# Gating GpSimd's v copy and relu(k) on VectorE's reciprocal and product of three heads back, with new instruction lists and more PE warm-up, in a linear-attention kernel

## The chip, the cores and the metric

The kernel runs on one core of one Trainium2 chip. The metric is device time in microseconds (us), the median of several executions. All comparisons below use runs that were marked as fast runs (e5 and e7 have one slow execution each, which is left out of their medians); where the profiled execution of a kernel fell in a slow run, the text says so. Engines are named as in the profile: PE is TensorE, DVE is VectorE, ACT is ScalarE, POOL is GpSimd, SP is the engine that issues the DMAs.

Each execution has a time and a span (first to last instruction), and in every execution of this case the time is 1.8 us above the span: 179.61 against 177.8 for the profiled execution of the kernel before, 187.68 against 185.9 for that of the changed one.

## The reference

Linear attention without a mask, 32 heads, sequence 2048, head size 128, bf16:

```python
def reference(q, k, v):                       # q, k, v: (1, 32, 2048, 128), bf16
    phi_q = jnp.where(q > 0, q + 1, jnp.exp(q)) + 1e-6
    phi_k = jnp.where(k > 0, k + 1, jnp.exp(k)) + 1e-6
    kv = jnp.einsum("bhsd,bhse->bhde", phi_k, v)
    z = jnp.einsum("bhsd->bhd", phi_k)
    num = jnp.einsum("bhqd,bhde->bhqe", phi_q, kv)
    den = jnp.einsum("bhqd,bhd->bhq", phi_q, z)[..., None] + 1e-6
    return num / den
```

The kernel uses phi(x) = (min(exp(x), 1) + eps) + relu(x), so that both parts go to PE as separate matmuls.

## The kernel before

Every operation has a name and a head number, and five lists give the order on each engine. The lists are what the scheduler would be in other kernels; an engine takes its list strictly in order, and semaphores are derived from the dependencies. The operations of head h that the argument needs are:

| name | engine | what | two-port mode |
|---|---|---|---|
| ek, eq | ACT | exp(k), exp(q transposed) | - |
| em | DVE | min(exp k, 1) + eps, 128x2048 bf16, SBUF to SBUF | yes |
| emq | DVE | the same for q | yes |
| rkd | DVE | relu(k), first half, 128x1024 bf16, SBUF to SBUF | yes |
| rqb | DVE | relu(q) second half, from PSUM | no |
| r.0, f.0 | DVE | reciprocal and product of 12 row tiles, from PSUM | no |
| r.1, f.1 | DVE | the same for the last 4 tiles | no |
| rkp | POOL | relu(k), second half, SBUF to SBUF | - |
| v1 | POOL | copy of v beside a column of ones, SBUF to SBUF | - |
| T, kv, n | PE | transpose of q; phi(k) times v; phi(q) times kv | - |

Code of the parts that the change and the argument touch (cuts are marked):

```python
WARM = (60, 30)                              # PE warm-up groups w0, w1
def kv_parts(h):
    return WHOLE                             # kv of a head is one operation
def gate(name, h):
    return []                                # no gates
# ... (lists: a stretch of DVE's, head 12 to 13)
#   ... r12.0 f12.0 emq13.0 rkd15.0 em15.0 r12.1 rqb14 f12.1 rkd16.0 r13.0 emq14.0 f13.0 ...
#   ... (POOL's: heads are swapped in places)
#   ... rkp15.0 rkp14.0 v115.0 rkp16.0 v117.0 v116.0 rkp17.0 rkp18.0 v119.0 v118.0 ...
for i, (a, b) in enumerate(rkp_parts(h)):
    add("POOL", f"rkp{h}.{i}", lambda e, a=a, b=b: e.tensor_scalar(
        rk_sb[:, h % NR, a:b], k_sb[:, h % NI, a:b], BIG, 0.0, op0=ALU.min, op1=ALU.max),
        over("ldk", h, k_parts, a, b) + freed(NR, h, ("kv", kv_parts)) + gate("rkp", h))
for i, (a, b) in enumerate(v_parts(h)):
    add("POOL", f"v1{h}.{i}", lambda e, a=a, b=b: e.tensor_copy(
        v1_sb[:, h % NV, a:b, 0:D].bitcast(i32), v_sb[:, h % NI, a:b].bitcast(i32)),
        [f"ldv{h}.{i}"] + freed(NV, h, ("kv", kv_parts)) + gate("v1", h))
# ... (f.0: the product, one input from PSUM)
e.tensor_tensor(out=..., in0=_ap(o_ps, ...), in1=_ap(rden_sb, ...), op=ALU.mult)
```

Without a gate, a POOL operation of head h waits for its load and for kv of head h - 2 (two buffers), so it starts when PE ends that kv.

Of the kernel before, what the change touches and what calls it, by code (L numbers as in the profile page):

```python
# [8 lines left out]
ENGINES = ("PE", "DVE", "ACT", "POOL", "SP")  # L9
NH = 32  # L10
NI, NO, NE, NR, NV, NQ, NK = 7, 12, 2, 2, 2, 2, 2
WARM = (60, 30)
HALVES = ((0, 8), (8, 16))
WHOLE = ((0, 16),)

# [6 lines left out]


def kv_parts(h):
    return WHOLE


RKP = (8, 8, 8, 8, 8, 8, 8, 8, 8, 8, 8, 8, 8, 8, 8, 8, 8, 8, 8, 8, 8, 8, 8, 8, 8, 8, 8, 8, 8, 8, 8, 8)
# [23 lines left out]


def gate(name, h):
    return []


ORDER = {
    "PE": """
        T0.0 T0.1 w1 w0 T1.0 kv0.0 kv1.0 n0.0 n0.1 T2.0 kv2.0 n1.0 T3.0 n1.1 kv3.0 n2.0 T4.0 n2.1 kv4.0 n3.0 T5.0  # L60
        n3.1 kv5.0 n4.0 T6.0 n4.1 kv6.0 n5.0 n5.1 T7.0 kv7.0 n6.0 T8.0 n6.1 kv8.0 n7.0 T9.0 n7.1 kv9.0 n8.0 T10.0
        n8.1 kv10.0 n9.0 T11.0 n9.1 kv11.0 n10.0 T12.0 n10.1 kv12.0 n11.0 T13.0 n11.1 kv13.0 n12.0 T14.0 n12.1
        kv14.0 n13.0 T15.0 n13.1 kv15.0 n14.0 T16.0 n14.1 kv16.0 n15.0 T17.0 n15.1 kv17.0 n16.0 n16.1 T18.0 kv18.0
        n17.0 T19.0 n17.1 kv19.0 n18.0 T20.0 n18.1 kv20.0 n19.0 T21.0 n19.1 kv21.0 n20.0 T22.0 n20.1 kv22.0 n21.0
        T23.0 n21.1 kv23.0 n22.0 T24.0 n22.1 kv24.0 n23.0 n23.1 T25.0 kv25.0 n24.0 T26.0 n24.1 kv26.0 n25.0 T27.0
        n25.1 kv27.0 n26.0 T28.0 n26.1 kv28.0 n27.0 T29.0 n27.1 kv29.0 n28.0 T30.0 n28.1 kv30.0 n29.0 T31.0 n29.1
        kv31.0 n30.0 n30.1 n31.1 n31.0 n31.2
    """,
    "DVE": """
        v1ones0 rkd0.0 em0.1 rkd1.0 rqb0 em0.0 eps0 em1.0 emq0.1 emq0.0 rqb1 v1ones1 eps1 rkd2.0 eps2 ones emq1.0  # L70
        rkd3.0 em2.0 r0.0 f0.0 em3.0 rqb2 r0.1 rkd4.0 f0.1 r1.0 emq2.0 f1.0 em4.0 rkd5.0 r1.1 rqb3 f1.1 r2.0 f2.0
        emq3.0 em5.0 rkd6.0 rqb4 r2.1 f2.1 r3.0 emq4.0 f3.0 em6.0 r3.1 rqb5 rkd7.0 f3.1 r4.0 emq5.0 f4.0 em7.0 r4.1
        f4.1 rqb6 r5.0 f5.0 emq6.0 rkd8.0 em8.0 r5.1 rqb7 f5.1 r6.0 emq7.0 f6.0 rkd9.0 em9.0 r6.1 rqb8 f6.1 r7.0
        emq8.0 f7.0 rkd10.0 em10.0 r7.1 rqb9 f7.1 r8.0 emq9.0 f8.0 rkd11.0 em11.0 r8.1 rqb10 f8.1 r9.0 rkd12.0 f9.0
        emq10.0 em12.0 r9.1 rqb11 f9.1 r10.0 f10.0 emq11.0 em13.0 rkd13.0 r10.1 rqb12 f10.1 rkd14.0 r11.0 emq12.0
# [137 lines left out]
def bass_standalone__linear_attn_elu__prompt_kernel(nc: bass.Bass, q: bass.AP, k: bass.AP, v: bass.AP, out: bass.AP):  # L213
# [11 lines left out]
    with ExitStack() as es:  # L225
# [73 lines left out]
        def head(h):  # L299
# [153 lines left out]
```

## Time and profile before

The kernel before took 176.82 us (median of 3).

These are lines of its page: the span, the busy time of the engines, the DMA rows of the 40 slices, and the shares of the chain of waits that ended last, by engine.

```profile
span 177.8 us, 6416 instructions
...
PE 161.9 (91%) x2842; PEld 158.1 (89%) x2842; DVE 158.4 (89%) x266; ACT 154.4 (87%) x131; POOL 71.5 (40%) x71
...
DMA  5999999999999999999999999999999945999973
GB/s 171 323 407 416 411 404 406 412 404 410 408 406 409 406 417 411 407 411 417 412 417 414 420 414 416 416 414 417 412 405 418 414 196 183 285 417 412 418 313 120
...
PE 43%; DVE 20%; DMA 18%; issue 5%; SPq 4%; ACT 4%; POOL 3%; DVEq 0%; POOLq 0%
```

DMA is full from the 3rd slice to the 32nd, has a hole from the 33rd to the 35th (142 to 156 us, deepest up to 152), and is full again for three slices. The chain runs through PE, DVE and DMA; no single engine owns it.

Next, the busy time of each engine in three stretches (us from the start; the columns are named in the first line).

```profile
core 0: us, PE busy (x) PEld busy (x) DVE busy (x) ACT busy (x) POOL busy (x), PEclk, DMA share, GB/s
31.00:78.00 47.00, 47.00 (x857) 46.77 (x855) 46.16 (x80) 47.00 (x40) 21.36 (x21) 1.00 1.03 409
78.00:126.00 48.00, 45.15 (x808) 44.13 (x806) 46.85 (x76) 44.83 (x38) 20.78 (x19) 1.00 1.03 415
142.00:152.00 10.00, 9.21 (x169) 9.11 (x168) 10.00 (x19) 9.04 (x8) 4.15 (x4) 1.00 0.59 202
```

From 31 to 78 us PE and ACT are busy the whole time and DVE 46.2 of 47 us. In this stretch eq starts every 4.72 us; this is the pace that PE and ACT set. From 78 to 126 us PE falls to 45.2 of 48.

The hole in DMA has its cause in the DMA list. This is SP's timeline at the place: the store of head 25 stood early in the list, and everything behind it waited 15.7 us.

```profile
132.63 15.72 SPq L388 DMA_DIRECT2D out_dram<-la  x2
```

The three two-port operations of DVE, by shape: count, then busy us and mean ns.

```profile
L311 DVE TENSOR_SCALAR la<-la 128x2048 bf16<-128x2048 bf16 x31 | 22.5, 725 | 1.7 <-ACT la L308 1.7
L345 DVE TENSOR_SCALAR la<-la 128x2048 bf16<-128x2048 bf16 x31 | 21.5, 694 | 0.4 <-ACT la L343 0.4
...
L314 DVE TENSOR_SCALAR la<-la 128x1024 bf16<-128x1024 bf16 x32 | 18.0, 566 | 7.4 <-DMA la<-in_k_dram 7.3
```

What these means hide is seen in the timeline. Below are DVE's operations at 90 us (start, duration, then the operation) and POOL's one at the same time. They are emq15, em17, rkd17 and r14.1, and on POOL rkp18.

```profile
89.46 0.68 DVE L345 TENSOR_SCALAR la<-la 128x2048 bf16<-128x2048 bf16 x1
90.06 0.69 DVE L311 TENSOR_SCALAR la<-la 128x2048 bf16<-128x2048 bf16 x1
90.66 1.26 DVE L314 TENSOR_SCALAR la<-la 128x1024 bf16<-128x1024 bf16 x1
91.85 0.17 DVE L373 RECIPROCAL la<-la 128x4 f32<-128x4 f32 x1
```

```profile
90.57 1.08 POOL L318 TENSOR_SCALAR la<-la 128x1024 bf16<-128x1024 bf16 x1 [2.31 <-PE la L329]
```

POOL's rkp18 came up while em17 ran, 0.09 us before rkd17 started. It went in first, and rkd17, which takes 0.33 us from its start to the next start when alone, took 1.19. I call an em, emq or rkd *blocked* if it was dispatched (its record in the trace begins) during a POOL operation and took over 0.15 us more than its usual start-to-start time (0.60 us, 0.33 us for the 1024-element ones). The kernel before has 11 of them, 7.5 us in all. The small table sums up what bounds it.

| | measured |
|---|---|
| pace of PE and ACT | 4.72 us per head |
| DVE's eight operations of a head, unblocked, start to start | 4.63 us |
| DVE's slack per head | under 0.1 us |
| blocked DVE operations | 11, 7.5 us |
| hole in DMA | 142 to 152 us, 202 GB/s in place of 410 |

### The profile page before, as it was taken

The page shows a single profiled execution, that of the slowest core. Times are in us where ns is not written, and L with a number is a line of the kernel's source. Part 1 is how long each engine was busy: PE and PEld are TensorE (multiplying, and loading weights), DVE is VectorE, ACT ScalarE, POOL GpSimd, SP SyncE. Part 2 cuts the span into 40 slices and gives each one's busy share as a digit, 9 for nine tenths or more (in the row PEclk, how much of TensorE's full clock was granted, in tenths as well). Part 3 has the DMA queues.
Part 4 walks back from the last instruction along what each step waited for, and adds up shares of the span by engine and source line. Part 5 has one row for each costly group of instructions (what it writes and reads, how often), then busy time and mean ns, then how long its engine had stood idle before and what let it go on. Part 6 is the DMA issues. An engine that isn't in the chain of part 4 may idle for free.

```text
span 177.8 us, 6416 instructions
## 1 busy us (share of the span) xinstructions
PE 161.9 (91%) x2842; PEld 158.1 (89%) x2842; DVE 158.4 (89%) x266; ACT 154.4 (87%) x131; POOL 71.5 (40%) x71
## 2 busy tenths in 40 slices
PE   2986999999999999999889999988999989999870
PEld 1976999999999999999789999978999889989770
DVE  0156899999999999998999999999999999989973
ACT  2599799999999999999898999978999979994600
POOL 1253818417454246262723626264256424360000
PEclk9999999999999999999999999999999999999968
DMA  5999999999999999999999999999999945999973
GB/s 171 323 407 416 411 404 406 412 404 410 408 406 409 406 417 411 407 411 417 412 417 414 420 414 416 416 414 417 412 405 418 414 196 183 285 417 412 418 313 120
DMA packets 19179, 67.52 MB, mean 380 GB/s; under 512 B 2128, under 2 KB 2512, under 8 KB 19152
## 3 DMA queue, kind: packets, MB, share of 16 engines
q1 hardware_dynamic: 19152, 67.12, 95.1%
q8 instruction: 22, 0.36, 0.8%
q14 instruction: 5, 0.04, 0.1%
HBM read 50.33 MB, written 16.78 MB: 377 GB/s over the span
## 4 chain that ended last, share of the span: by engine, by line
PE 43%; DVE 20%; DMA 18%; issue 5%; SPq 4%; ACT 4%; POOL 3%; DVEq 0%; POOLq 0%
PE la L329 17%; DMA la<-in_k_dram 11%; PE la L364 9%; PE la L366 8%; PE la L340 8%; DVE la L380 8%; DMA out_dram<-la 7%; SPq L296 4%; DVE la L314 4%; DVE la L311 3%; DVE la L352 2%; ACT la L343 2%; DVE la L345 2%; POOL la L318 2%; POOL la L322 2%
## 5 line engine op out<-in xcount | busy, mean ns | idle before, releaser
L380 DVE TENSOR_TENSOR la<-la 128x1536 bf16<-128x1536 f32 (+2 forms) x65 | 77.7, 1199 | 2.0 <-DMA out_dram<-la 1.4
L366 PE MATMUL la<-la 128*128 128x129 bf16 x512 | 69.2, 222 | 0.0
L364 PE MATMUL la<-la 128*128 128x129 bf16 x512 | 69.1, 221 | 0.0
L329 PE MATMUL la<-la 128*128 128x129 bf16 x1024 | 64.0, 219 | 2.0 <-ACT la L349 1.4
L343 ACT ACTIVATE la<-la 128x2048 bf16<-128x2048 bf16 (+1 forms) x33 | 60.1, 1825 | 6.5 <-PE la L366 6.0
L308 ACT ACTIVATE la<-la 128x2048 bf16<-128x2048 bf16 (+1 forms) x33 | 61.3, 1860 | 2.1 <-DMA la<-in_k_dram 1.9
L329 PEld LDWEIGHTS la<-la 128*128 128x128 bf16 x1024 | 59.9, 97 | 2.7 <-DVE la L278 1.5
L318 POOL TENSOR_SCALAR la<-la 128x1024 bf16<-128x1024 bf16 x32 | 36.1, 1137 | 44.1 <-PE la L329 33.5
L322 POOL COPY la<-la 128x1024 int32<-128x1024 int32 (+1 forms) x33 | 35.3, 1076 | 44.0 <-PE la L329 22.4
L366 PEld LDWEIGHTS la<-la 128*128 128x128 bf16 x512 | 50.0, 98 | 0.0
L364 PEld LDWEIGHTS la<-la 128*128 128x128 bf16 x512 | 47.8, 98 | 0.0
L340 PE MATMUL la<-la 128*128 128x128 bf16 x512 | 34.8, 222 | 7.0 <-DMA la<-in_q_dram 3.6
L340 PEld LDWEIGHTS la<-la 128*128 128x128 bf16 x512 | 29.6, 99 | 9.0 <-issue 4.0
L359 PE MATMUL la<-la 128*128 128x3 bf16 (+1 forms) x192 | 32.6, 170 | 2.5 <-DVE la L380 2.5
L349 ACT ACTIVATE la<-la 128x1024 bf16<-128x1024 bf16 x32 | 32.6, 1019 | 2.5 <-PE la L340 2.5
L311 DVE TENSOR_SCALAR la<-la 128x2048 bf16<-128x2048 bf16 (+1 forms) x33 | 23.3, 706 | 3.1 <-ACT la L308 3.1
L314 DVE TENSOR_SCALAR la<-la 128x1024 bf16<-128x1024 bf16 x32 | 18.0, 566 | 7.4 <-DMA la<-in_k_dram 7.3
L345 DVE TENSOR_SCALAR la<-la 128x2048 bf16<-128x2048 bf16 (+1 forms) x33 | 22.3, 677 | 0.4 <-ACT la L343 0.4
L359 PEld LDWEIGHTS la<-la 128*128 128x128 bf16 x192 | 18.9, 99 | 3.5 <-DVE la L380 3.1
L352 DVE TENSOR_SCALAR la<-la 128x1024 bf16<-128x1024 bf16 x32 | 21.3, 667 | 0.7 <-ACT la L343 0.7
L373 DVE RECIPROCAL la<-la 128x12 f32<-128x12 f32 (+2 forms) x65 | 12.8, 198 | 2.2 <-PE la L366 1.4
L334 ACT ACTIVATE la<-la 128x129 bf16<-128x129 f32 x32 | 9.0, 281 | 1.0 <-PE la L329 1.0
(14 smaller groups left out, 13.5 us busy)
## 6 DMA issues: line engine op xcount, KB each, us to landing
la<-in_k_dram SPq DMA_DIRECT2D x31, 512.0 KB, 13.9
la<-in_q_dram SPq DMA_DIRECT2D x31, 512.0 KB, 13.9
la<-in_v_dram SPq DMA_DIRECT2D x31, 512.0 KB, 13.3
out_dram<-la SPq DMA_DIRECT2D x31, 512.0 KB, 13.2
la<-in_q_dram SPq DMA_DIRECT2D x2, 256.0 KB, 3.0
la<-in_k_dram SPq DMA_DIRECT2D x2, 256.0 KB, 5.2
la<-in_v_dram SPq DMA_DIRECT2D x2, 256.0 KB, 7.6
out_dram<-la SPq DMA_DIRECT2D x2, 192.0 KB, 2.1
```

The source lines that it names most:

```text
L308: add("ACT", f"ek{h}.{i}", lambda e, a=a, b=b: e.activation(em_sb[:, h % NE, a:b], k_sb[:, h % NI, a:b], ACT.Exp), [f"ldk{h}.{i}"] + freed ...
L311: add("DVE", f"em{h}.{i}", lambda e, a=a, b=b: e.tensor_scalar(em_sb[:, h % NE, a:b], em_sb[:, h % NE, a:b], 1.0, EPS, op0=ALU.min, op1=AL ...
L318: add("POOL", f"rkp{h}.{i}", lambda e, a=a, b=b: e.tensor_scalar(rk_sb[:, h % NR, a:b], k_sb[:, h % NI, a:b], BIG, 0.0, op0=ALU.min, op1=A ...
L322: add("POOL", f"v1{h}.{i}", lambda e, a=a, b=b: e.tensor_copy(v1_sb[:, h % NV, a:b, 0:D].bitcast(i32), v_sb[:, h % NI, a:b].bitcast(i32)), ...
L329: ins = e.matmul(kv_ps, lhsT=src[:, j], rhs=v1_sb[:, h % NV, j, 0:NC], start=(j + part == 0), stop=(j == NT - 1 and part == 1))
L340: ins = e.transpose(xT[:, j], q_sb[:, h % NI, j], ident[:])
L343: add("ACT", f"eq{h}.{i}", lambda e, a=a, b=b: e.activation(emq_sb[:, h % NQ, a:b], xT[:, a:b], ACT.Exp), [f"T{h}.{i}"] + freed(NQ, h, ("n ...
L349: add("ACT", f"rqa{h}", lambda e: e.activation(rq_sb[:, h % NQ, 0:n], xT[:, 0:n], ACT.Relu), over("T", h, q_parts, 0, n) + freed(NQ, h, (" ...
L359: e.matmul(_ap(o_ps[:, :], o + D, [[NC, m]]), lhsT=ones[:], rhs=epsr[:, 0:m], start=True, stop=False, skip_group_check=True)
L364: e.matmul(to, lhsT=emq_sb[:, h % NQ, t], rhs=kvs_sb[:, h % NK], start=False, stop=False, skip_group_check=True)
L366: ins = e.matmul(to, lhsT=rq_sb[:, h % NQ, t], rhs=kvs_sb[:, h % NK], start=False, stop=True, skip_group_check=True)
L380: return e.tensor_tensor(out=_ap(o_sb[:, :, :, :], first(o_sb[:, h % NO, t0, 0:1]) - first(o_sb[:, :, :, :]), [[m * D, nb], [D, m], [1, D] ...
```

## The change

Intent: let GpSimd work while VectorE reads PSUM. The v copy of head h now waits for r.0 of head h - 3, just before the long product f.0; relu(k) waits for f.0. The instruction lists were made anew for that (ACT's, not shown, changes only in heads 0 to 2 and 21), kv was halved, and four short warm-up groups of PE replace one of 30. The diff, cut to its core:

```diff
-WARM = (60, 30)
+WARM = (60, 15, 15, 15, 15)
 def kv_parts(h):
-    return WHOLE
+    return HALVES
 def gate(name, h):
-    return []
+    if h < 3:
+        return []
+    return [f"r{h - 3}.0"] if name == "v1" else [f"f{h - 3}.0"]
 ORDER = {
   "PE":                                        # (cut: kv halves, n0.0 before kv1)
-        T0.0 T0.1 w1 w0 T1.0 kv0.0 kv1.0 n0.0 n0.1 T2.0 kv2.0 n1.0 T3.0 n1.1 ...
+        w3 w4 T0.0 w1 T0.1 w2 w0 T1.0 kv0.0 kv0.1 n0.0 kv1.0 kv1.1 n0.1 T2.0 ...
   "DVE":                                       # (cut: heads 11 to 13 of 32)
-        ... r11.0 emq12.0 f11.0 em14.0 r11.1 rqb13 f11.1 r12.0 f12.0 emq13.0 rkd15.0 em15.0 r12.1 rqb14 f12.1 ...
+        ... r11.0 rkd14.0 emq12.0 f11.0 em14.0 r11.1 rqb13 f11.1 r12.0 emq13.0 f12.0 rkd15.0 em15.0 rkd16.0 rqb14 ...
   "POOL":                                      # (cut: now in the order of heads)
-        ... rkp15.0 rkp14.0 v115.0 rkp16.0 v117.0 v116.0 rkp17.0 ...
+        ... rkp14.0 v115.0 rkp15.0 v116.0 rkp16.0 v117.0 rkp17.0 ...
   "SP":                                        # (cut: stores and loads nearly in the order of heads)
-        ... st15.0 ldk30.0 st17.0 ldv29.0 ldq29.0 st18.0 st25.0 ldv30.0 ldk31.0 st16.0 ldv31.0 st21.0 ldq31.0 ...
+        ... st14.0 st15.0 ldv29.0 ldk30.0 ldq30.0 ldk31.0 ldq31.0 st16.0 ldv30.0 st17.0 ldv31.0 st18.0 st19.0 ...
```

More of the change, by code (lines that the diff above doesn't have):

```diff
@@ L54, in gate @@
 def gate(name, h):
-    return []
+    if h < 3:
+        return []
+    return [f"r{h - 3}.0"] if name == "v1" else [f"f{h - 3}.0"]
 ORDER = {
     "PE": """
-        T0.0 T0.1 w1 w0 T1.0 kv0.0 kv1.0 n0.0 n0.1 T2.0 kv2.0 n1.0 T3.0 n1.1 kv3.0 n2.0 T4.0 n2.1 kv4.0 n3.0 T5.0
-        n3.1 kv5.0 n4.0 T6.0 n4.1 kv6.0 n5.0 n5.1 T7.0 kv7.0 n6.0 T8.0 n6.1 kv8.0 n7.0 T9.0 n7.1 kv9.0 n8.0 T10.0
-        n8.1 kv10.0 n9.0 T11.0 n9.1 kv11.0 n10.0 T12.0 n10.1 kv12.0 n11.0 T13.0 n11.1 kv13.0 n12.0 T14.0 n12.1
-        kv14.0 n13.0 T15.0 n13.1 kv15.0 n14.0 T16.0 n14.1 kv16.0 n15.0 T17.0 n15.1 kv17.0 n16.0 n16.1 T18.0 kv18.0
-        n17.0 T19.0 n17.1 kv19.0 n18.0 T20.0 n18.1 kv20.0 n19.0 T21.0 n19.1 kv21.0 n20.0 T22.0 n20.1 kv22.0 n21.0
-        T23.0 n21.1 kv23.0 n22.0 T24.0 n22.1 kv24.0 n23.0 n23.1 T25.0 kv25.0 n24.0 T26.0 n24.1 kv26.0 n25.0 T27.0
-        n25.1 kv27.0 n26.0 T28.0 n26.1 kv28.0 n27.0 T29.0 n27.1 kv29.0 n28.0 T30.0 n28.1 kv30.0 n29.0 T31.0 n29.1
-        kv31.0 n30.0 n30.1 n31.1 n31.0 n31.2
+        w3 w4 T0.0 w1 T0.1 w2 w0 T1.0 kv0.0 kv0.1 n0.0 kv1.0 kv1.1 n0.1 T2.0 kv2.0 kv2.1 n1.0 T3.0 n1.1 kv3.0 kv3.1
+        n2.0 T4.0 n2.1 kv4.0 kv4.1 n3.0 n3.1 T5.0 kv5.0 kv5.1 n4.0 T6.0 n4.1 kv6.0 kv6.1 n5.0 T7.0 n5.1 kv7.0 kv7.1
+        n6.0 T8.0 n6.1 kv8.0 kv8.1 n7.0 T9.0 n7.1 kv9.0 kv9.1 n8.0 T10.0 n8.1 kv10.0 kv10.1 n9.0 T11.0 n9.1 kv11.0
+        kv11.1 n10.0 T12.0 n10.1 kv12.0 kv12.1 n11.0 T13.0 n11.1 kv13.0 kv13.1 n12.0 T14.0 n12.1 kv14.0 kv14.1 n13.0
+        T15.0 n13.1 kv15.0 kv15.1 n14.0 T16.0 n14.1 kv16.0 kv16.1 n15.0 T17.0 n15.1 kv17.0 kv17.1 n16.0 T18.0 n16.1
+        kv18.0 kv18.1 n17.0 T19.0 n17.1 kv19.0 kv19.1 n18.0 T20.0 n18.1 kv20.0 kv20.1 n19.0 T21.0 n19.1 kv21.0
+        kv21.1 n20.0 T22.0 n20.1 kv22.0 kv22.1 n21.0 T23.0 n21.1 kv23.0 kv23.1 n22.0 T24.0 n22.1 kv24.0 kv24.1 n23.0
+        T25.0 n23.1 kv25.0 kv25.1 n24.0 T26.0 n24.1 kv26.0 kv26.1 n25.0 n25.1 T27.0 kv27.0 kv27.1 n26.0 T28.0 n26.1
+        kv28.0 kv28.1 n27.0 T29.0 n27.1 kv29.0 kv29.1 n28.0 T30.0 n28.1 kv30.0 kv30.1 n29.0 n29.1 T31.0 kv31.0
+        kv31.1 n30.0 n30.1 n31.0 n31.1 n31.2
@@ L68 @@
     """,
     "DVE": """
-        v1ones0 rkd0.0 em0.1 rkd1.0 rqb0 em0.0 eps0 em1.0 emq0.1 emq0.0 rqb1 v1ones1 eps1 rkd2.0 eps2 ones emq1.0
-        rkd3.0 em2.0 r0.0 f0.0 em3.0 rqb2 r0.1 rkd4.0 f0.1 r1.0 emq2.0 f1.0 em4.0 rkd5.0 r1.1 rqb3 f1.1 r2.0 f2.0
-        emq3.0 em5.0 rkd6.0 rqb4 r2.1 f2.1 r3.0 emq4.0 f3.0 em6.0 r3.1 rqb5 rkd7.0 f3.1 r4.0 emq5.0 f4.0 em7.0 r4.1
-        f4.1 rqb6 r5.0 f5.0 emq6.0 rkd8.0 em8.0 r5.1 rqb7 f5.1 r6.0 emq7.0 f6.0 rkd9.0 em9.0 r6.1 rqb8 f6.1 r7.0
-        emq8.0 f7.0 rkd10.0 em10.0 r7.1 rqb9 f7.1 r8.0 emq9.0 f8.0 rkd11.0 em11.0 r8.1 rqb10 f8.1 r9.0 rkd12.0 f9.0
@@ L75 @@
-        emq10.0 em12.0 r9.1 rqb11 f9.1 r10.0 f10.0 emq11.0 em13.0 rkd13.0 r10.1 rqb12 f10.1 rkd14.0 r11.0 emq12.0
-        f11.0 em14.0 r11.1 rqb13 f11.1 r12.0 f12.0 emq13.0 rkd15.0 em15.0 r12.1 rqb14 f12.1 rkd16.0 r13.0 emq14.0
-        f13.0 em16.0 r13.1 rqb15 f13.1 r14.0 f14.0 emq15.0 em17.0 rkd17.0 r14.1 rqb16 f14.1 r15.0 rkd18.0 f15.0
-        emq16.0 em18.0 r15.1 f15.1 rqb17 r16.0 f16.0 emq17.0 em19.0 rkd19.0 r16.1 rqb18 f16.1 r17.0 emq18.0 f17.0
-        rkd20.0 em20.0 r17.1 rqb19 f17.1 r18.0 f18.0 emq19.0 rkd21.0 em21.0 r18.1 rqb20 f18.1 r19.0 emq20.0 f19.0
@@ L80 @@
-        em22.0 rkd23.0 rkd22.0 rqb21 r19.1 r20.0 f19.1 f20.0 emq21.0 em23.0 rkd24.0 rqb22 r20.1 f20.1 r21.0 emq22.0
-        f21.0 em24.0 rqb23 r21.1 f21.1 r22.0 emq23.0 rkd25.0 f22.0 em25.0 r22.1 f22.1 rqb24 r23.0 f23.0 emq24.0
-        rkd26.0 em26.0 r23.1 rqb25 f23.1 r24.0 emq25.0 f24.0 em27.0 rkd27.0 r24.1 rqb26 f24.1 r25.0 emq26.0 f25.0
-        rkd28.0 em28.0 r25.1 rqb27 f25.1 r26.0 emq27.0 f26.0 rkd29.0 em29.0 r26.1 rqb28 f26.1 r27.0 emq28.0 f27.0
-        rkd30.0 em30.0 r27.1 rqb29 f27.1 r28.0 f28.0 emq29.0 rkd31.0 em31.0 rqb30 r28.1 f28.1 r29.0 emq30.0 f29.0
@@ L85 @@
-        emq31.0 r29.1 rqb31 r30.0 f29.1 f30.0 r30.1 f30.1 r31.1 f31.1 r31.0 r31.2 f31.0 f31.2
+        eps0 rkd0.0 emq0.1 rkd1.0 v1ones0 rqb0 eps1 ones em0.0 em0.1 emq0.0 em1.0 v1ones1 eps2 r0.0 rkd2.0 rqb1 f0.0
+        em2.0 rkd3.0 emq1.0 em3.0 rkd4.0 r0.1 rqb2 f0.1 r1.0 f1.0 emq2.0 em4.0 rqb3 r1.1 f1.1 rkd5.0 r2.0 emq3.0
+        f2.0 em5.0 r2.1 f2.1 rqb4 r3.0 emq4.0 f3.0 rkd6.0 em6.0 rqb5 r3.1 f3.1 r4.0 emq5.0 f4.0 rkd7.0 em7.0 r4.1
+        rqb6 f4.1 r5.0 f5.0 emq6.0 em8.0 rkd8.0 r5.1 rqb7 f5.1 r6.0 rkd9.0 emq7.0 f6.0 em9.0 rqb8 r6.1 f6.1 r7.0
@@ new lines @@
+        rkd10.0 f7.0 emq8.0 em10.0 rqb9 r7.1 f7.1 r8.0 rkd11.0 emq9.0 f8.0 em11.0 r8.1 rqb10 f8.1 rkd12.0 r9.0
+        emq10.0 f9.0 em12.0 rqb11 r9.1 f9.1 rkd13.0 r10.0 emq11.0 f10.0 em13.0 r10.1 rqb12 f10.1 r11.0 rkd14.0
+        emq12.0 f11.0 em14.0 r11.1 rqb13 f11.1 r12.0 emq13.0 f12.0 rkd15.0 em15.0 rkd16.0 rqb14 r12.1 f12.1 r13.0
+        emq14.0 f13.0 em16.0 rkd17.0 rqb15 r13.1 f13.1 r14.0 emq15.0 f14.0 em17.0 rqb16 r14.1 f14.1 rkd18.0 r15.0
+        emq16.0 f15.0 em18.0 r15.1 rqb17 f15.1 r16.0 rkd19.0 emq17.0 f16.0 em19.0 rqb18 r16.1 f16.1 r17.0 emq18.0
@@ new lines @@
+        f17.0 rkd20.0 em20.0 r17.1 rqb19 f17.1 r18.0 rkd21.0 f18.0 emq19.0 em21.0 rqb20 r18.1 f18.1 r19.0 rkd22.0
+        emq20.0 f19.0 em22.0 rqb21 r19.1 f19.1 r20.0 rkd23.0 emq21.0 f20.0 em23.0 r20.1 rqb22 f20.1 emq22.0 r21.0
+        rkd24.0 f21.0 em24.0 r21.1 rqb23 f21.1 r22.0 emq23.0 f22.0 em25.0 rkd25.0 r22.1 rqb24 f22.1 r23.0 rkd26.0
+        f23.0 emq24.0 em26.0 r23.1 rqb25 f23.1 rkd27.0 r24.0 f24.0 emq25.0 em27.0 r24.1 f24.1 rqb26 r25.0 emq26.0
+        f25.0 rkd28.0 em28.0 rqb27 r25.1 f25.1 emq27.0 r26.0 rkd29.0 f26.0 em29.0 r26.1 rqb28 f26.1 r27.0 f27.0
@@ L86 @@
+        emq28.0 rkd30.0 r27.1 rqb29 f27.1 r28.0 em30.0 emq29.0 f28.0 r28.1 f28.1 rqb30 em31.0 rkd31.0 r29.0 f29.0
+        emq30.0 rqb31 r29.1 emq31.0 f29.1 r30.0 f30.0 r30.1 f30.1 r31.0 f31.0 r31.1 f31.1 r31.2 f31.2
     """,
     "ACT": """
-        rqa0 ek0.1 ek0.0 eq0.1 eq0.0 ek1.0 eq1.0 kvs0 rqa1 ek2.0 kvs1 ek3.0 eq2.0 kvs2 rqa2 ek4.0 eq3.0 kvs3 rqa3
+        rqa0 eq0.0 eq0.1 ek0.0 ek0.1 ek1.0 eq1.0 kvs0 ek2.0 rqa1 kvs1 ek3.0 eq2.0 kvs2 rqa2 ek4.0 eq3.0 kvs3 rqa3
         ek5.0 eq4.0 kvs4 rqa4 ek6.0 eq5.0 kvs5 rqa5 ek7.0 eq6.0 kvs6 rqa6 ek8.0 eq7.0 kvs7 rqa7 ek9.0 eq8.0 kvs8
@@ L92 @@
         ek18.0 eq17.0 kvs17 rqa17 ek19.0 eq18.0 kvs18 rqa18 ek20.0 eq19.0 kvs19 rqa19 ek21.0 eq20.0 kvs20 rqa20
-        ek22.0 eq21.0 rqa21 kvs21 ek23.0 eq22.0 kvs22 rqa22 ek24.0 eq23.0 kvs23 rqa23 ek25.0 eq24.0 kvs24 rqa24
+        ek22.0 eq21.0 kvs21 rqa21 ek23.0 eq22.0 kvs22 rqa22 ek24.0 eq23.0 kvs23 rqa23 ek25.0 eq24.0 kvs24 rqa24
         ek26.0 eq25.0 kvs25 rqa25 ek27.0 eq26.0 kvs26 rqa26 ek28.0 eq27.0 kvs27 rqa27 ek29.0 eq28.0 kvs28 rqa28
@@ L97 @@
     "POOL": """
-        ident0 ident rkp0.0 rkp1.0 v10.1 v10.0 v11.0 v12.0 rkp2.0 rkp3.0 v13.0 v14.0 rkp5.0 rkp4.0 v15.0 rkp6.0
-        v16.0 v17.0 v18.0 rkp7.0 rkp8.0 rkp9.0 v19.0 rkp10.0 v110.0 rkp11.0 v111.0 v112.0 rkp13.0 rkp12.0 v113.0
-        v114.0 rkp15.0 rkp14.0 v115.0 rkp16.0 v117.0 v116.0 rkp17.0 rkp18.0 v119.0 v118.0 rkp19.0 rkp20.0 v121.0
-        v120.0 rkp21.0 v122.0 rkp23.0 rkp22.0 v123.0 rkp24.0 v124.0 v125.0 v126.0 rkp25.0 rkp26.0 rkp27.0 v127.0
-        rkp28.0 v128.0 rkp29.0 v129.0 rkp30.0 rkp31.0 v130.0 v131.0
+        ident0 ident rkp0.0 v10.0 v10.1 rkp1.0 v11.0 v12.0 rkp2.0 rkp3.0 v13.0 v14.0 rkp4.0 v15.0 rkp5.0 v16.0
@@ L103 @@
+        rkp6.0 v17.0 rkp7.0 v18.0 rkp8.0 v19.0 rkp9.0 v110.0 rkp10.0 v111.0 rkp11.0 v112.0 rkp12.0 v113.0 rkp13.0
+        v114.0 rkp14.0 v115.0 rkp15.0 v116.0 rkp16.0 v117.0 rkp17.0 v118.0 rkp18.0 v119.0 rkp19.0 v120.0 rkp20.0
+        v121.0 rkp21.0 v122.0 rkp22.0 v123.0 rkp23.0 v124.0 rkp24.0 v125.0 rkp25.0 v126.0 rkp26.0 v127.0 rkp27.0
+        v128.0 rkp28.0 rkp29.0 v129.0 rkp30.0 v130.0 v131.0 rkp31.0
     """,
     "SP": """
-        ldq0.0 ldq0.1 ldk0.0 ldk0.1 ldk1.0 ldq1.0 ldv0.1 ldv0.0 ldv1.0 ldk2.0 ldv2.0 ldk3.0 ldq2.0 ldv3.0 ldq3.0
@@ L106 @@
-        ldk4.0 ldq8.0 ldv4.0 ldk5.0 ldq4.0 ldv5.0 ldk6.0 ldk7.0 ldq5.0 ldv6.0 ldq6.0 ldv8.0 ldk8.0 ldv7.0 ldq7.0
-        ldk9.0 ldq9.0 ldk11.0 ldq12.0 ldq11.0 ldv9.0 ldk10.0 ldq10.0 ldk14.0 ldv10.0 ldq13.0 ldk15.0 ldk12.0 ldv11.0
-        ldk13.0 ldv13.0 ldv12.0 ldv15.0 ldv14.0 st0.0 ldq14.0 ldq17.0 ldq16.0 ldv16.0 ldq15.0 ldq18.0 ldk16.0
-        ldq19.0 ldv20.0 ldv17.0 ldk18.0 st1.0 st2.0 ldk17.0 st4.0 ldk19.0 ldv19.0 ldv18.0 st3.0 ldv21.0 ldv22.0
-        st5.0 st6.0 st10.0 ldk20.0 ldk22.0 ldv23.0 ldq20.0 ldk21.0 ldq21.0 st9.0 ldk23.0 st7.0 ldq22.0 st8.0 ldq23.0
@@ L111 @@
-        ldk24.0 ldv25.0 ldq26.0 ldq27.0 ldk25.0 ldv24.0 ldk26.0 ldq24.0 st11.0 ldk27.0 ldv26.0 ldq28.0 ldq25.0
-        st14.0 ldq30.0 st12.0 ldv27.0 ldk28.0 st13.0 ldk29.0 ldv28.0 st15.0 ldk30.0 st17.0 ldv29.0 ldq29.0 st18.0
-        st25.0 ldv30.0 ldk31.0 st16.0 ldv31.0 st21.0 ldq31.0 st23.0 st20.0 st24.0 st27.0 st26.0 st28.0 st19.0 st22.0
-        st29.0 st30.0 st31.1 st31.0 st31.2
+        ldk0.0 ldq0.0 ldq0.1 ldk0.1 ldk1.0 ldv0.0 ldq1.0 ldv0.1 ldv1.0 ldk2.0 ldv2.0 ldk3.0 ldq2.0 ldq3.0 ldk4.0
@@ new lines @@
+        ldv3.0 ldv4.0 ldk5.0 ldq4.0 ldv5.0 ldq5.0 ldk6.0 ldk7.0 ldv6.0 ldq6.0 ldv7.0 ldq7.0 ldv8.0 ldk8.0 ldq8.0
+        ldk9.0 ldk10.0 ldv9.0 ldk11.0 ldv10.0 ldq9.0 st0.0 ldq10.0 ldq11.0 ldq12.0 ldq13.0 ldv11.0 st1.0 ldq14.0
+        ldk12.0 ldk13.0 ldv12.0 ldq15.0 ldk14.0 ldk15.0 ldv13.0 ldk16.0 ldv14.0 ldv15.0 st2.0 ldq16.0 ldk17.0
+        ldv16.0 st3.0 ldq17.0 ldv17.0 ldq18.0 ldq19.0 ldk18.0 st4.0 ldk19.0 ldv18.0 ldv19.0 ldq20.0 st5.0 ldv20.0
+        ldk20.0 ldk21.0 ldq21.0 st6.0 ldk22.0 ldq22.0 st7.0 ldv21.0 ldk23.0 ldk24.0 ldv22.0 ldk25.0 st8.0 st9.0
@@ L115 @@
+        ldv23.0 ldk26.0 ldv24.0 st10.0 ldq23.0 st11.0 ldq24.0 ldv25.0 ldv26.0 ldq25.0 st12.0 ldq26.0 ldq27.0 st13.0
+        ldk27.0 ldv27.0 ldq28.0 ldk28.0 ldv28.0 ldk29.0 ldq29.0 st14.0 st15.0 ldv29.0 ldk30.0 ldq30.0 ldk31.0
+        ldq31.0 st16.0 ldv30.0 st17.0 ldv31.0 st18.0 st19.0 st20.0 st21.0 st22.0 st23.0 st24.0 st25.0 st26.0 st27.0
+        st28.0 st29.0 st30.0 st31.0 st31.1 st31.2
     """,
```

## The prediction

> **What bounds it now.** In the busy-time windows from 31 to 78 us, PE, ACT and DVE are busy 47.0, 47.0 and 46.2 of 47 us, and the start of eq moves by 4.72 us per head: PE and ACT are full, and DVE has under 0.1 us of slack per head (its eight operations take 0.14+1.67+0.12+0.60 (r, f), 0.59 (rqb), 0.60 (em), 0.58 (emq), 0.33 (rkd) = 4.63 us, start to next start in the timeline). Later heads are slower: eq 4 starts at 30.8 and eq 31 at 164.2, 5.7 us more than 27 x 4.72. The chain of waits there runs through DVE, through a store that frees f13's buffer only at 83.5, and through k31, which lands at 156.9: the DMA queue sat 15 us on one store (head 25), and DMA fell to 0.45 for 10 us.
>
> **The port.** The Trainium skill ("SBUF — State Buffer", Who interferes with whom) says VectorE's two-port modes and GpSimd hold one port pair exclusively, whoever issues first. The trace agrees: of 12 em/emq/rkd dispatched while a GpSimd operation ran, 11 stretched until it ended (rkd 0.33 to 1.2, em/emq 0.6 to 1.0), 7.5 us in total, while r, f and rqb never stretched. A GpSimd operation that comes up during one such DVE operation goes in before the next (rkd17 behind em17, rkd22 behind rkd23).
>
> **What the change does.**
> 1. The DMA list becomes nearly ordered. Counting 1.27 us per 512 KB ahead of each transfer (estimate from 412 GB/s), loads come in time. Gain 2.5 to 4 us.
> 2. Gates: the v copy (1.04) starts behind r.0, relu(k) (1.04) behind f.0. DVE's next operation after f.0 is always em, emq or rkd. Where only one stands there, relu(k) waits for it and then runs under r.1, rqb, f.1: free. In the new list two or more stand after f.0 in 15 heads, and two stand between r.0 and f.0 in 7: GpSimd goes between them and the second waits about 0.9 us. That is 22 x 0.9 = 20 us of DVE time (estimate) in place of 7.5, against under 3 us of slack in all.
> 3. 30 more warm-up matmuls at 60 ns: 1.8 us more in a wait: no effect. Halved kv: only semaphores.
>
> **Sum.** Without blocked operations: eq 2 at 20.9 (q2 lands 19.7, same place in the list), plus 29 x 4.73, plus 12.5 of tail: span 170.6, time about 170. DVE's own sum: r0.0 at about 16.5, plus 145.5 us of work, plus 17 to 20 of blocked time, gives 180 to 182 for the last product, span about 183 to 185; the time is about 1 us less than the span, as before. Some blocks may hide in the DMA-bound start. I take 182.0 us, 171 to 188: slower, unless the blocks don't happen, in which case clearly faster. Chances: faster 0.22, within 2% 0.23, slower 0.55.
>
> **What would show it.** Right: after the start the mean of rkd or em well above 566 and 725 ns, DVE with no idle time and at 97% or more while PE and ACT fall below 90%; chain mostly DVE; heads 11-13, 16-20, 22-25 at some 5.5 us, heads 9, 10, 14, 15 at 4.73. DMA without the hole at 142 to 152 us. Wrong: em at 0.68 and rkd at 0.42 us nearly everywhere, chain PE and ACT, period 4.73: then 170 to 172.
>
> **What would make it wrong.** GpSimd losing to back-to-back DVE operations; late v loads; the ordered DMA list being worth more.

## More of the kernel before

The experiments ran on three chips, e1 to e8 on one, e9 to e12 on a second, e13 to e15 on a third; the kernel before, measured on each, has fast medians of 177.3, 177.4 and 177.9 us there.

The profiled execution is one of several, and need not be a typical one.

## The result

The changed kernel took 188.61 us (median of 4, 187.43 to 189.64). Ratio to the kernel before: 1.062, interval 1.051 to 1.074. Here and below a ratio is the mean time of one kernel's fast runs over that of the other's of the same rounds, so it is not quite the ratio of the medians. The change made the kernel 6.2% slower; the predicted 182.0 us (range 171 to 188) has the direction and misses the size, and the measured median lies just outside the range.

The page of the changed kernel, the lines that answer to those shown of before:

```profile
span 185.9 us, 6520 instructions
...
PE 165.1 (89%) x2872; PEld 159.6 (86%) x2872; DVE 168.9 (91%) x266; ACT 155.3 (84%) x131; POOL 82.4 (44%) x71
...
DMA  5999999999999999999999999999999999622235
GB/s 151 323 417 409 406 410 407 405 411 406 413 415 414 407 410 419 414 409 418 415 416 413 388 395 378 414 417 416 417 410 421 412 418 413 271 90 117 105 149 191
...
DVE 63%; PE 13%; issue 11%; ACT 11%; POOL 0%; DVEq 0%; POOLq 0%
```

DVE now has 63% of the chain. The hole from the 33rd slice on is gone, but the 35th moves 271 GB/s and from the 36th on DMA moves 90 to 190: it ran ahead and waits for products to store.

The stretches; the last one is where DMA starts to run dry.

```profile
core 0: us, PE busy (x) PEld busy (x) DVE busy (x) ACT busy (x) POOL busy (x), PEclk, DMA share, GB/s
31.00:78.00 47.00, 43.11 (x769) 41.85 (x767) 46.62 (x72) 42.73 (x37) 23.49 (x19) 1.00 1.03 411
78.00:126.00 48.00, 43.72 (x780) 42.45 (x777) 47.64 (x73) 43.35 (x37) 23.46 (x18) 1.00 1.02 407
152.00:164.00 12.00, 11.56 (x208) 11.21 (x206) 11.93 (x19) 10.97 (x9) 5.02 (x5) 1.00 0.85 342
```

DVE is busy 46.6 of 47 us and 47.6 of 48, PE has fallen to 43.1 and 43.7. The three two-port operations:

```profile
L315 DVE TENSOR_SCALAR la<-la 128x2048 bf16<-128x2048 bf16 x31 | 30.3, 978 | 0.8 <-ACT la L312 0.8
L349 DVE TENSOR_SCALAR la<-la 128x2048 bf16<-128x2048 bf16 x31 | 26.3, 849 | 0.0
...
L318 DVE TENSOR_SCALAR la<-la 128x1024 bf16<-128x1024 bf16 x32 | 16.1, 502 | 2.6 <-DMA la<-in_k_dram 2.6
```

em went from a mean of 725 to 978 ns and emq from 694 to 849, while rkd fell from 566 to 502. The two waits of POOL that are the gates (total us, times, longest):

```profile
POOL la L322 <- DVE la L384: 37.4, 28, 4.7
POOL la L326 <- DVE la L377: 37.4, 26, 2.5
```

And the place where the time goes, at head 12. DVE's timeline shows r12.0, emq13, f12.0, rkd15, em15, rkd16, rqb14; POOL's shows v1 of head 15 and rkp15:

```profile
81.98 0.21 DVE L377 RECIPROCAL la<-la 128x12 f32<-128x12 f32 x1
82.12 0.62 DVE L349 TENSOR_SCALAR la<-la 128x2048 bf16<-128x2048 bf16 x1
82.67 1.74 DVE L384 TENSOR_TENSOR la<-la 128x1536 bf16<-128x1536 f32 x1
84.33 0.41 DVE L318 TENSOR_SCALAR la<-la 128x1024 bf16<-128x1024 bf16 x1
84.66 1.52 DVE L315 TENSOR_SCALAR la<-la 128x2048 bf16<-128x2048 bf16 x1
86.10 0.41 DVE L318 TENSOR_SCALAR la<-la 128x1024 bf16<-128x1024 bf16 x1
86.44 0.68 DVE L356 TENSOR_SCALAR la<-la 128x1024 bf16<-128x1024 bf16 x1
```

```profile
82.26 1.37 POOL L326 COPY la<-la 128x1024 int32<-128x1024 int32 x1 [0.57 <-DVE la L377]
84.49 1.15 POOL L322 TENSOR_SCALAR la<-la 128x1024 bf16<-128x1024 bf16 x1 [0.85 <-DVE la L384]
```

v1 did what was intended: it was released by r12.0, waited for emq13 and ran under f12.0. rkp15 was released by f12.0's end, at 84.49, when DVE was 0.16 us into rkd15. It waited for rkd15 and then went in before em15, which took 1.44 us from start to start in place of 0.60. In the whole kernel 23 operations were blocked, 18.9 us in all, against 11 and 7.5 us before.

Two pages of the Trainium skill say why these operations and not others. "SBUF — State Buffer", Who interferes with whom: GpSimd and VectorE's two-port modes hold one shared port pair exclusively, and who issues first has it for a whole instruction. "VectorE: DVE Perf Modes", The perf-mode tier table: a bf16 tensor_scalar in SBUF runs at four elements per cycle, and an operand in PSUM caps an operation at two or one. The trace fits both: em takes 0.60 us from start to start for 2048 elements and f.0 1.66 us for 1536, and r, f and rqb never stretched under POOL (f.0's marked duration has a mean of 1.74 us with POOL running beside it and 1.75 without).

### The profile page after: what moved, and what is told of

Read it like the earlier page. It is cut to its first block, busy times and chain, and to the rows that moved or that the text cites. A ratio compares the mean times of both kernels' runs of the same rounds, so it can differ in the third digit from the quotient of the medians.

```text
span 185.9 us, 6520 instructions
## 1 busy us (share of the span) xinstructions
PE 165.1 (89%) x2872; PEld 159.6 (86%) x2872; DVE 168.9 (91%) x266; ACT 155.3 (84%) x131; POOL 82.4 (44%) x71
## 4 chain that ended last, share of the span: by engine, by line
DVE 63%; PE 13%; issue 11%; ACT 11%; POOL 0%; DVEq 0%; POOLq 0%
DVE la L384 28%; DVE la L349 11%; DVE la L356 8%; ACT la L347 7%; DVE la L315 7%; DVE la L318 5%; PE la L291 5%; DVE la L377 4%; PE la L344 3%; PE la L368 2%; PE la L370 2%; ACT la L312 2%; ACT la L353 1%; ACT la L338 1%; PE la L363 1%
## 5 line engine op out<-in xcount | busy, mean ns | idle before, releaser
L347 ACT ACTIVATE la<-la 128x2048 bf16<-128x2048 bf16 (+1 forms) x33 | 60.2, 1825 | 15.7 <-PE la L370 11.2
L370 PE MATMUL la<-la 128*128 128x129 bf16 x512 | 68.0, 220 | 0.0
L368 PE MATMUL la<-la 128*128 128x129 bf16 x512 | 67.9, 219 | 0.0
L333 PE MATMUL la<-la 128*128 128x129 bf16 x1024 | 64.0, 219 | 0.0
L322 POOL TENSOR_SCALAR la<-la 128x1024 bf16<-128x1024 bf16 x32 | 43.0, 1343 | 46.4 <-DVE la L384 37.4
L326 POOL COPY la<-la 128x1024 int32<-128x1024 int32 (+1 forms) x33 | 38.9, 1179 | 41.8 <-DVE la L377 37.4
L349 DVE TENSOR_SCALAR la<-la 128x2048 bf16<-128x2048 bf16 (+1 forms) x33 | 27.4, 830 | 5.0 <-ACT la L347 5.0
L315 DVE TENSOR_SCALAR la<-la 128x2048 bf16<-128x2048 bf16 (+1 forms) x33 | 31.1, 945 | 0.8 <-ACT la L312 0.8
L356 DVE TENSOR_SCALAR la<-la 128x1024 bf16<-128x1024 bf16 x32 | 21.3, 667 | 0.2 <-ACT la L347 0.2
L318 DVE TENSOR_SCALAR la<-la 128x1024 bf16<-128x1024 bf16 x32 | 16.1, 502 | 2.6 <-DMA la<-in_k_dram 2.6
L291 PE MATMUL la<-la 128*128 128x120 bf16 x120 | 9.1, 251 | 1.5 <-POOL la L277 1.5
```

The lines of the kernel that those rows point to most:

```text
L315: add("DVE", f"em{h}.{i}", lambda e, a=a, b=b: e.tensor_scalar(em_sb[:, h % NE, a:b], em_sb[:, h % NE, a:b], 1.0, EPS, op0=ALU.min, op1=AL ...
L333: ins = e.matmul(kv_ps, lhsT=src[:, j], rhs=v1_sb[:, h % NV, j, 0:NC], start=(j + part == 0), stop=(j == NT - 1 and part == 1))
L347: add("ACT", f"eq{h}.{i}", lambda e, a=a, b=b: e.activation(emq_sb[:, h % NQ, a:b], xT[:, a:b], ACT.Exp), [f"T{h}.{i}"] + freed(NQ, h, ("n ...
L349: add("DVE", f"emq{h}.{i}", lambda e, a=a, b=b: e.tensor_scalar(emq_sb[:, h % NQ, a:b], emq_sb[:, h % NQ, a:b], 1.0, EPS, op0=ALU.min, op1 ...
L368: e.matmul(to, lhsT=emq_sb[:, h % NQ, t], rhs=kvs_sb[:, h % NK], start=False, stop=False, skip_group_check=True)
L370: ins = e.matmul(to, lhsT=rq_sb[:, h % NQ, t], rhs=kvs_sb[:, h % NK], start=False, stop=True, skip_group_check=True)
```

## The experiments

Theory 1: the loss is the blocked time. A gate that opens at the end of r.0 or f.0 lets POOL come up during DVE's next two-port operation; if a second one stands behind it, POOL goes in between and the second is blocked. Theory 2: the new lists, the halved kv or the warm-up are slow by themselves. Theory 3: the gates cost because they make POOL late. Counts of blocked operations in the text are from the profiled execution of each kernel, counted as above. e5 and e7 have one slow execution each, which is left out of their medians.

### e1: the changed kernel without its gates

```diff
 def gate(name, h):
-    if h < 3:
-        return []
-    return [f"r{h - 3}.0"] if name == "v1" else [f"f{h - 3}.0"]
+    return []
```

> The changed kernel with the gates taken out and everything else (lists, halves, warm-up) kept. Theory 1 (the gates bring GpSimd in between two back-to-back VectorE operations that use two ports): blocked VectorE time falls from 19 us to under 8 us and the time to 171 to 176 us. Theory 2 (the new instruction lists, the halved kv or the warm-up are what is slow): the time stays within 2% of 188 us.

Measured: 184.95 us, ratio 1.041 (1.035 to 1.048). Blocked: 25 operations, 14.2 us. Theory 1 as I had put it failed here: taking the gates out gives back 3.7 of 11.5 us, not all of it. What did not fail is the tie between blocked time and time. Without gates POOL starts at the end of a kv, and with the new lists this falls into em, emq or rkd as often as with the gates, though for a shorter part of each. So neither "the gates" nor "the lists" alone can be the answer, and the next runs change the place of the two to each other.

### e2: gates kept, the runs behind them broken up

Only DVE's list is edited, at 21 places like this one; where a run held emq, this stays, as PE needs it first.

```diff
-  r12.0 emq13.0 f12.0 rkd15.0 em15.0 rkd16.0 rqb14 r12.1 f12.1 r13.0
+  r12.0 emq13.0 f12.0 em15.0 rqb14 r12.1 f12.1 rkd15.0 rkd16.0 r13.0
```

> The changed kernel with its gates, but in VectorE's list the second and third of the em/emq/rkd that stood together behind a gating r.0 or f.0 are moved behind f.1 (21 places). Theory 1: nothing is left to be blocked, under 3 us of blocked time, period 4.73 us, time 171 to 176 us. Theory 3 (the gates cost by making GpSimd, and so kv, late, whatever VectorE does next): stays above 184 us.

Measured: 176.28 us, ratio 0.994 (0.987 to 1.001). Blocked: 3 operations, 2.0 us, all before 21 us. That is 12.3 us less than the changed kernel, by moving operations on one engine; the gates and every other list are the same. Theory 3 falls, since the gates are still there. The time is just above what theory 1 expected (171 to 176), since some heads still took 5.0 us. In its trace PE's weight loads for n waited 5 times for an emq (1.8 us) and 9 times for a product (4.4 us); that the moved operations delay these is read from the list and not shown by a run.

### e5 and e6: only one of the two kinds of run broken up

e5 breaks up the 14 runs behind f.0 and leaves the 7 behind r.0; e6 does the reverse (the edits are those of e2, for half of the places).

> The changed kernel with its gates; only the 14 runs of em/emq/rkd behind f.0 are broken up, the 7 behind r.0 stay. Theory 1 counts blocked operations: 7 are left, about 0.85 us each, so about 6 us on top of the 2 us of the version with none left; DVE's slack hides little: 180 to 183 us. If the number of such runs is not what sets the time, it is near 176 or near 188 us.

> The same with the 7 runs behind r.0 broken up and the 14 behind f.0 left. Theory 1: about 14 blocked operations, about 12 us on top of 2, time 183 to 186 us, that is clearly more than with the 7 left.

| kernel | blocked after 25 us | blocked time after 25 us | time, us | ratio |
|---|---|---|---|---|
| e2, no run left | 0 | 0 | 176.28 | 0.994 |
| e5, 7 runs behind r.0 left | 7 | 5.9 | 182.25 | 1.032 |
| e6, 14 runs behind f.0 left | 14 | 11.9 | 183.67 | 1.034 |
| the changed kernel | 21 | 17.8 | 188.61 | 1.062 |

The count of blocked operations is as expected in both, one for each run left. Both times are about where theory 1 put them, but "clearly more" with 14 than with 7 was wrong: the difference is 1.4 us by the medians, and the intervals of the ratios overlap. A run behind r.0 costs 6.0 / 7 = 0.9 us, one behind f.0 at most 7.4 / 14 = 0.5 us; at most, because e6 also has six blocked operations before 25 us (3.9 us), where e5 has two (1.7) and e2 three (2.0). In the 7 places it is emq that is blocked in front of f.0, and the next n on PE needs both emq and f.0; this ordering is read from the lists and no run isolates it.

### e9: the lists untouched, the gates moved behind the runs

```diff
+BEHIND = {..., 11: ("emq12.0", "f11.0"), 12: ("r12.0", "rkd16.0"), 13: ("r13.0", "rkd17.0"), ...}
 def gate(name, h):
     if h < 3:
         return []
-    return [f"r{h - 3}.0"] if name == "v1" else [f"f{h - 3}.0"]
+    return [BEHIND[h - 3][0 if name == "v1" else 1]]
```

> The changed kernel with all its lists as they are; only the gates move: where several em/emq/rkd stand together behind r.0 or f.0 (21 places from head 1 on, and head 0), GpSimd waits for the last of them in place of r.0 or f.0. Theory 1: no operation is left for GpSimd to come in before, blocked time under 3 us from head 3 on, 174 to 178 us with the list untouched. Theory 2 (the list itself is slow): stays above 184 us.

Measured: 173.38 us, ratio 0.980 (0.972 to 0.987), which leaves open whether it is 2% faster than the kernel before; a repeat with 5 rounds (e15, below) took 173.15 us, and its ratio of 0.974 (0.969 to 0.979) settles it: faster. Blocked: 3 operations, 0.7 us. This is the plainest test of the mechanism: no operation is moved on any engine, rkp15 starts 1.35 us behind f12.0's end in place of 0.09 us, and the kernel is 15 us faster than the changed one. Its DVE and POOL at head 12, of the same operations as above emq13, rkd15, em15, rkd16, rqb14, and v1 of head 15 and rkp15:

```profile
76.29 0.63 DVE L352 TENSOR_SCALAR la<-la 128x2048 bf16<-128x2048 bf16 x1
...
78.50 0.42 DVE L321 TENSOR_SCALAR la<-la 128x1024 bf16<-128x1024 bf16 x1
78.83 0.69 DVE L318 TENSOR_SCALAR la<-la 128x2048 bf16<-128x2048 bf16 x1
79.43 0.42 DVE L321 TENSOR_SCALAR la<-la 128x1024 bf16<-128x1024 bf16 x1
79.77 0.68 DVE L359 TENSOR_SCALAR la<-la 128x1024 bf16<-128x1024 bf16 x1
```

```profile
76.43 1.38 POOL L329 COPY la<-la 128x1024 int32<-128x1024 int32 x1 [0.74 <-DVE la L380]
79.93 1.04 POOL L325 TENSOR_SCALAR la<-la 128x1024 bf16<-128x1024 bf16 x1 [2.12 <-DVE la L321]
```

rkp15 is released at rkd16's end, starts with rqb14 and runs under operations that read PSUM; em15 takes 0.60 us again. The page shows what bounds the kernel now:

```profile
span 171.6 us, 6511 instructions
...
PE 161.6 (94%) x2872; PEld 158.8 (93%) x2872; DVE 152.1 (89%) x266; ACT 153.5 (89%) x131; POOL 75.8 (44%) x71
...
PE 71%; ACT 15%; DVE 7%; DMA 3%; issue 1%; SPq 0%; DVEq 0%
```

PE has 71% of the chain and DVE 7%; eq starts every 4.7 us in nearly all heads from 7 on.

### e3 and e10: the kernel before with gates

e3 adds only the gate function. e10 also puts POOL's list in the order of heads (the list of the changed kernel).

> The kernel before with nothing but the gates added. Its VectorE list has two or more em/emq/rkd behind f.0 in 22 heads and behind r.0 in 1. Theory 1: about 23 blocked operations of about 0.85 us, blocked time near 20 us, time 185 to 190 us. Theory 2: within 2% of 177 us.

> The kernel before with the gates and with GpSimd's list in the order of the changed kernel, as the kernel before has heads swapped in it (v of 17 before v of 16), which makes a gate wait for a later head. If those swaps made the 215 us of the first try: GpSimd and 'issue' leave the chain, VectorE takes it, 20 to 24 blocked operations, 186 to 194 us. If not, it stays above 205 us.

e3 measured 214.91 us, far over both expectations: I had overlooked that POOL's old list has heads swapped. v1 of 17 stands before v1 of 16, so with a gate POOL waits for r.0 of head 14 while kv of head 16 needs the v1 behind it; in the same way relu(k) of 15, which waits for f.0 of head 12, stands before relu(k) of 14. The table of waits (total us, times, longest) shows POOL waiting for f.0 and PE for relu(k), which is L320 there:

```profile
POOL la L320 <- DVE la L382: 81.6, 18, 7.6
...
PE la L331 <- POOL la L320: 17.4, 6, 3.9
```

e10 measured 189.34 us, ratio 1.072 (1.062 to 1.082), 28 blocked operations, 22.2 us, and DVE has 74% of the chain. So the gates, with POOL's list put in order for them, cost the kernel before 12 us as well, and the blocked operations are again the kind that the mechanism names: its DVE list has two or more of em, emq and rkd behind f.0 in 22 heads. Without gates that list does no harm from 31 to 78 us, as POOL's starts fall in other places there.

### e7, e8 and e11: a regular list, with and without gates

e8 goes further than e2: from head 3 on DVE's list is the same for every head, and PE's three irregular places (heads 3, 25, 29) are made regular. e7 is e2 without gates, e11 is e8 without gates (gate returns an empty list).

```diff
+  r{h}.0 emq{h+1} f{h}.0 em{h+3} r{h}.1 rqb{h+2} f{h}.1 rkd{h+4}      # e8, for each h
```

> VectorE's list with the 21 runs broken up, and no gates. If the list alone cures it: 174 to 178 us and under 5 us of blocked time. If, without the gates, GpSimd (started by the end of kv) drifts into em, emq and rkd wherever they stand, as it did in the changed kernel without gates (25 blocked, 14.4 us): 15 or more blocked operations, and 180 to 185 us.

> A version meant to beat both: the gates kept, and VectorE's list made the same for every head from head 3 on (r.0, emq, f.0, em, r.1, rqb, f.1, rkd), so that one two-port operation stands behind each gate; PE's three irregular places (heads 3, 25, 29) made regular. Theory 1: under 3 us of blocked time, every head at 4.72 to 4.75 us, so about 0.13 us x 27 less than with the 21 runs broken up alone: 171.5 to 174 us.

> The version with the regular VectorE list, without gates. If the gates carry the gain: GpSimd drifts as in the list with the 21 runs broken up, 15 or more blocked, 180 to 187 us. If the regular list is enough: 173 to 176 us.

| DVE list | with gates, us | without gates, us |
|---|---|---|
| of the changed kernel | 188.61 | 184.95 |
| runs broken up (e2, e7) | 176.28 | 185.91 |
| regular (e8, e11) | 173.72 | 187.44 |

e8 has 5 blocked operations (2.9 us); its ratio to the kernel before is 0.978 (0.973 to 0.983), faster, but unclear against the line of 2%. e7 has 30 (17.2 us) and e11 30 (19.4 us); the profiled execution of e7 was a slow one, so of it only the count is used. In e11 heads take 4.7 and 5.8 us in turn. One of its blocked operations, em15 behind f12.0, with the v1 that PE's kv released:

```profile
85.47 1.53 DVE L314 TENSOR_SCALAR la<-la 128x2048 bf16<-128x2048 bf16 x1
```

```profile
85.42 1.04 POOL L325 COPY la<-la 128x1024 int32<-128x1024 int32 x1 [2.49 <-PE la L332]
```

POOL was 0.05 us ahead of em15. This answers whether the gates have a use: with a list that suits them they are worth 10 to 14 us, and a list without runs does not replace them. It also shows that the intent of the change was right and that the place of the gates spoilt it.

### e4 and e12: the DMA list alone

e4 is the kernel before with the new DMA list; e12 is e8 with the old DMA list.

> The kernel before with nothing but the new DMA list. If the DMA hole and the late store and load are worth what I predicted: 2.5 to 4 us faster, 173 to 174.5 us, and no DMA slice under 90% between 5 and 165 us. If the hole was hidden by VectorE's pace: within 1% of 177 us.

> The version with the regular VectorE list and the gates, with the DMA list of the kernel before. My prediction valued the new DMA list at 2.5 to 4 us: then 176 to 178 us, with the hole in DMA back. In the kernel before, the new list cost 3.3 us, with 10 blocked operations among the first heads; if that loss was the port's and not the list's, the list is worth something here. If the list is worth nothing: within 0.5% of 173.7 us.

e4 measured 180.57 us, ratio 1.014 (1.007 to 1.022): slower by some 1.4%, against the expected gain. (Three of its four executions show a clock of 0.986 or 0.987, against one of seven of the kernel before beside it; the one at 0.998 took 178.61 us. So the median may overstate the loss.) The hole is gone (the 33rd to 35th slice at 421, 414 and 412 GB/s), but 15 operations were blocked (8.7 us), 10 of them before 62 us, and eq of head 9 starts at 57.6 us in place of 54.5. From head 9 to head 31 e4 is the faster one: eq of 31 starts 107.2 us after eq of 9, against 109.6. So the list gains 2.4 us there and loses 3.1 in the first nine heads. Blocked time before 62 us is 5.2 us against 2.4; that other arrival times of loads moved POOL's starts into DVE's two-port operations is a likely reason, which no run isolates. e12 measured 176.13 us (174.74 to 177.34) against 173.72 for e8, on another chip. With the port quiet in both, the new list is worth about 2.4 us, with runs that scatter by more than 1%. So the value of a DMA list was not a number of its own: in the kernel before the first heads took it back.

### e13, e14, e15: warm-up and halved kv

All three start from e9. e13 has the old warm-up (`WARM = (60, 30)`, `T0.0 T0.1 w1 w0 T1.0`), e14 has kv whole, e15 is e9 again as their control on the same chip, with 5 rounds.

> The version with the gates behind the runs, with the warm-up of the kernel before (60 and 30, both behind head 0's transposes). I predicted no effect of the extra warm-up: within 0.7% of 173.4 us. If the warm-up had a part in the loss: 1 us or more faster; if it helps: 1 us or more slower, and the PE clock or the start of the first heads shows it.

> The same version with kv in one piece per head in place of two halves (31 heads have one v part and one k part, so only head 0 can gain from halves). Predicted no effect: within 0.7% of 173.4 us.

> Control for the two others on the same chip, and an interval with 5 rounds for the version that beat both kernels: 172.5 to 174.5 us, 1.5 to 2.7% under the kernel before.

| kernel | time, us | ratio to before | interval |
|---|---|---|---|
| e13, old warm-up | 174.64 | 0.983 | 0.978 to 0.988 |
| e14, kv whole | 172.50 | 0.972 | 0.967 to 0.978 |
| e15, control | 173.15 | 0.974 | 0.969 to 0.979 |

The old warm-up is 1.5 us slower by the medians (the intervals overlap). In its trace all 90 warm-up matmuls stand in one block of 6.0 us between T0.1 and T1, and T1 starts at 13.3 us; in the control 30 of them ran before the first q had landed and T1 starts at 12.1. These are single traces: e9, the same program as the control, starts T1 at 11.2, so executions of one kernel differ by 0.9 us here. The new warm-up seems to help a little, and with the gates behind the runs it had no part in the loss; that its place is the reason is not shown. Whole kv is 0.65 us faster by the medians, within what the runs scatter. e14, the gates behind the runs with kv whole, has the lowest median found.

## Why the prediction was wrong

Point by point, as the prediction put it:

1. **"What bounds it now"** held: PE and ACT at 4.72 us per head, DVE with under 0.1 us of slack. The remark that the time is "about 1 us less than the span, as before" was wrong, see 5.
2. **"22 x 0.9 = 20 us of DVE time"** held: 23 blocked operations and 18.9 us. The heads held too. A blocked operation behind the gates of head h shows in the step from eq of head h + 2 to eq of head h + 3: it is 4.7 us for the unblocked heads 9, 10, 14 and 15, 5.5 for 11, 12 and 13, and 5.2 to 5.8 for 16 to 20 and 22 to 25.
3. **DVE's own sum** held nearly: r0.0 starts at 16.6 us (predicted 16.5), the work after it is 164.8 us (145.5 + 17 to 20 = 162.5 to 165.5), DVE idles 1.8 us (predicted none), and the last product ends at 183.3 (predicted 180 to 182).
4. **"Gain 2.5 to 4 us"** of the DMA list was not there for the kernel before as a whole (e4: 3.3 us slower by the medians, though 2.4 us faster from head 9 to 31) and about 2.4 us where the port is quiet (e12). In the sum above it does not enter, as DVE's work sets the end.
5. **The mechanism was right; the step that failed is the last term of the sum, from span to time.** The span was put at 183 to 185 and measured 185.9. The prediction then took off 1 us, by comparing the span of one profiled execution (177.8) with the median of other executions (176.8). That execution itself took 179.61 us; the right step is to add 1.8. This is 2.8 us of the 6.6 that were missed. Another 1.9 us is the span against the middle of 183 to 185, most of it the 1.8 us that DVE idles. The changed kernel's other runs had spans up to 187.8, which is 0.9 more in the median. The last 1 us was taken off by choice, for "some blocks may hide", and none did after 25 us: all 21 runs behind gates there were blocked.
6. **"Warm-up and halved kv: no effect"** held to within 1.5 us and 0.65 us (e13, e14), and the warm-up's sign is a small gain.
7. The signs named for "right" appeared, with two misses: PE and ACT fell to 92 and 91% from 31 to 78 us, not below 90%, and DVE was not without idle time. Of "rkd or em" it was em whose mean rose; rkd's fell, as mostly em and emq were the second of a run.

What the prediction did not look at is e1: it counted the blocks that the gates make, and I then expected that without gates the new lists would have few. They have 25. In the kernel before, each of POOL's 20 starts from 31 to 78 us came during an operation that reads PSUM or during the last two-port operation of a run (v1 of 18 during em7, before r4.1, say), which is what e9 makes the rule. Why the old lists keep that phase and the new ones lose it was not settled by a run.

## What to carry to other kernels

When GpSimd is released by a VectorE operation, look at what VectorE does next: release it behind the last two-port operation of a run, so that it starts together with one that reads PSUM, and not one operation earlier. Where both engines are nearly full, the place of the gates was worth 15 us here with the lists untouched (173 us against 189). Without gates three new lists took 185 to 187 us (e1, e7, e11), and a new DMA list alone lost 3 us in the first nine heads (e4). Before adding up a prediction, check how span and time of the *same* execution differ.

## What the Trainium skill lacked or had wrong

- "SBUF — State Buffer", Who interferes with whom, says that issue order decides and the loser waits for a whole instruction. It lacks what happens in a run: a GpSimd operation that comes up during one two-port operation goes in before the next one, even when that stands right behind. All 21 runs of the changed kernel behind a gate after 25 us lost this way, with em and emq at 1.45 us in place of 0.60 and rkd at 1.18 in place of 0.33.
- The same page, in its summary of rules for kernel authors, advises to "Schedule whichever is off the critical path". It lacks that the release point can do this: with GpSimd released by f.0 the kernel took 188.6 us, released by the last two-port operation behind f.0 it took 173.4, with the same lists (e9, the v copy's gates moved likewise).
- "VectorE: DVE Perf Modes", Side-by-side, gives about 693 ns for 2048 bf16 elements in the fastest mode. The marked duration agrees (0.68 us), but operations that follow each other without a wait started every 0.60 us; for adding up a full engine the smaller number is the right one. The page's section on the errata has a formula that gives about 594 ns, and says that it under-predicts the duration of one operation; it lacks that this is the spacing of operations that follow each other.
- "TensorE: Matmul & The Clock Gate", What's actually happening, counts the warm-up budget in time, some 3.4 us, and not in matmuls, and calls it variable from run to run. The traces bear out that the count is not fixed, but the time varied widely too: with the same start of PE's list, matmuls followed each other at some 101 to 107 ns for 2.8 us (e15, 28 matmuls), 3.8 us (e9, 36) and 5.9 us (the changed kernel, 57) from the first one on, and at 53 to 56 ns afterwards. So 3.4 us is not an upper limit. The page lacks that warm-up matmuls can delay real ones: in e13 T1 started only as the block of 90 in front of it ended, 13.3 us, with its PSUM buffer free from 10.3 us on.
